# Squared-ReLU attention and adapter mixture on one core: a list scheduler writes the order of every engine, and PSUM is handed out by the bank

## The chip, the core and the metric

The kernel runs on one core of a Trainium2 chip. The metric is the device time in microseconds (us) of one execution. TensorE (PE) multiplies and transposes into PSUM, ScalarE (ACT) and VectorE (DVE) read PSUM and write SBUF, GpSimd (POOL) issues the input transfers and SyncE (SP) the output transfers. PSUM has 8 banks of 512 fp32 values per partition.

## The reference, cut to what matters

```python
# q, k, v: (8, 12, 448, 64); w_gate: (768, 8); A: (8, 768, 16); B: (8, 16, 768)
scores = (1 / sqrt(64)) * q @ k.T            # per batch and head, 448 x 448
attn = maximum(scores, 0) ** 2 / 448
x = (attn @ v), heads side by side           # (3584, 768)
logits = x @ w_gate                          # 8 experts, the best 2 count
w = softmax over the best 2
out = x + sum over the 2 experts of w_e * (x @ A[e]) @ B[e]
```

## The kernel before

Work comes in 8 batches of 3 "quads"; a quad is four heads of one batch, two of them (`g`) on each half of the 128 partitions and two (`sl`) side by side. Sequence positions are split as (p j), so that a step `j` of 7 takes 64 of the 448 keys for all four heads. There are 24 x 7 = 168 steps. A step is:

- `emit_qk(n)` (L228): four 64x64 matmuls of 448 columns into a score tile `s` of two PSUM banks. `ps_s` holds two such tiles.
- `emit_relu(n)` (L238): one ACT instruction over both banks, 128x896, writes `a1`; L240: one DVE product squares it into `a2`.
- `emit_pv(n)` (L252): four matmuls that add `a2` times `v` to `oT`, two banks that are held for the whole quad.

Before a quad, `job_transpose` turns its q and its k (14 PE transposes, L112, and a DVE copy, L119, each). After a quad, `emit_xt` copies `oT` into `xt` (L262 on ACT, L263 on DVE). When the columns of 128 rows are complete, `job_moe` runs for two or three of the 28 row tiles at once: gate logits and the 128 adapter columns `z` (L133), eight short DVE and ACT instructions that make the weights (L145 to L161), `zp` (L166), its transpose `zt` (L175) and copy `zT` (L180), and then for each tile two pieces of output, `o`: identity matmuls that bring `x` itself into the bank (L189), an fp32 matmul with B (L197), a copy to SBUF (512 columns on ACT, L208; 256 on DVE, L210) and two stores by SP (L212).

The order of every engine is the order in which Python emits the instructions. The loop over n at the end fixes it: in step n PE gets QK(n), then a transpose job or one piece of `job_moe`, and then PV(n-2) (`LAG` is 2). In PSUM `misc` has two banks for the transposes and all of `job_moe`, `s` four and `oT` two. What the loop emits, each engine runs strictly in that order, and an instruction waits for the semaphores of what it reads and overwrites.

Loads are issued by POOL, batch 0 by pairs of heads, each later batch as a whole when its buffer comes free. A is loaded by six transfers in runs of 16 floats.

Of the kernel before, what the change touches and what calls it, by code (L numbers as in the profile page):

```python
# [15 lines left out]
PH = 64  # L16


@with_exitstack
def kernel(  # L20
# [21 lines left out]
    NC_ = HH // 2  # L42
    scale = 1.0 / math.sqrt(Dh)
# [3 lines left out]
    loads = ctx.enter_context(tc.tile_pool(name="loads", bufs=3))  # L47
    tpool = ctx.enter_context(tc.tile_pool(name="tpool", bufs=2))
    apool = ctx.enter_context(tc.tile_pool(name="apool", bufs=4))
    mpool = ctx.enter_context(tc.tile_pool(name="mpool", bufs=2))  # L50
    opool = ctx.enter_context(tc.tile_pool(name="opool", bufs=4))
# [8 lines left out]
    identb = const.tile([128, 128], BF16)  # L60

# [5 lines left out]
    )  # L67

    batches = {}

    def load_batch(b, per_quad=False):
        tiles = [
            loads.tile([128, HH, J * Dh], BF16, name=f"{nm}n{b}", tag=f"{nm}n") for nm in "qkv"
        ]
        batches[b] = tiles
        parts = [(2 * c, 2 * c + 2) for c in range(NC_)] if per_quad else [(0, HH)]
        for s0, s1 in parts:
            for t, src in zip(tiles, (qv, kv, vv)):
                for g in range(2):
                    nc.gpsimd.dma_start(  # L80
                        out=t[g * PH : g * PH + PH, s0:s1, :], in_=src[b, g, :, s0:s1, :]
                    )
# [3 lines left out]
    load_batch(0, per_quad=True)  # L86
    nc.sync.dma_start(out=B_sb, in_=moe_B.rearrange("e r d -> (e r) d"))
    load_batch(1)
    nc.gpsimd.dma_start(
        out=awg[:, :, RE:ZW], in_=moe_w_gate.rearrange("(do di) e -> di do e", di=128)  # L90
    )
    for do in range(DO):
        nc.gpsimd.dma_start(
            out=awg[:, do, 0:RE].rearrange("p (e r) -> p e r", e=E),
            in_=moe_A[:, do * 128 : do * 128 + 128, :].transpose([1, 0, 2]),
        )

    quads = [(b, c) for b in range(B) for c in range(NC_)]
    NQ = len(quads)
    qkT = {}  # L100

    def misc(name):
        return ps_m.tile([128, 512], F32, name=name, tag="misc")


    def job_transpose(qi, which):
        b, c = quads[qi]
        src = batches[b][which]
        ps = ps_m.tile([128, J * 128], BF16, name=f"tp{which}_{qi}", tag="misc")
        for j in range(J):  # L110
            for sl in range(2):
                nc.tensor.transpose(  # L112
                    ps[sl * PH : sl * PH + PH, j * 128 : j * 128 + 128],
                    src[:, 2 * c + sl, j * Dh : j * Dh + Dh],
                    identb,
                )
        yield
        sb = tpool.tile([128, J, 2, PH], BF16, name=f"{'qk'[which]}T{qi}", tag=f"{'qk'[which]}T")
        nc.vector.tensor_copy(sb.rearrange("p j a s -> p (j a s)"), ps)  # L119
        qkT[qi, which] = sb  # L120

    def out_rows(m, bp):

        b = 2 * bp + m // J
        return out[b * S : b * S + S, :].rearrange("(p j) f -> j p f", j=J)[m % J]

    def job_moe(bp, tiles_):
        T = len(tiles_)
        c0 = [bp * 2 * S + 128 * i for i in tiles_]
        z = misc(f"z{bp}_{tiles_[0]}")  # L130
        for t in range(T):
            for do in range(DO):
                nc.tensor.matmul(  # L133
                    out=z[:, t * ZW : t * ZW + ZW],
                    lhsT=xt[:, do, c0[t] : c0[t] + 128],
                    rhs=awg[:, do, :],
                    start=(do == 0),
                    stop=(do == DO - 1),
                )
        yield  # L140
        z3 = z[:, : T * ZW].rearrange("p (t w) -> p t w", t=T)
        lg = z3[:, :, RE:ZW]
        mx = mpool.tile([128, 3, 8], F32, name=f"mx{bp}_{tiles_[0]}", tag="mx")
        for t in range(T):
            nc.vector.max(mx[:, t, :], z[:, t * ZW + RE : t * ZW + ZW])  # L145
        sub = mpool.tile([128, 3, E], F32, name=f"sub{bp}_{tiles_[0]}", tag="sub")
        nc.vector.tensor_tensor(
            sub[:, :T], lg, mx[:, :T, 0:1].to_broadcast([128, T, E]), op=ALU.subtract
        )
        w = mpool.tile([128, 3, E], F32, name=f"w{bp}_{tiles_[0]}", tag="w")  # L150
        nc.scalar.activation(w[:, :T], sub[:, :T], ACTF.Exp)
        mask = mpool.tile([128, 3, E], F32, name=f"mask{bp}_{tiles_[0]}", tag="mask")
        nc.vector.tensor_tensor(
            mask[:, :T], lg, mx[:, :T, 1:2].to_broadcast([128, T, E]), op=ALU.is_ge
        )
        yield
        nc.vector.tensor_mul(w[:, :T], w[:, :T], mask[:, :T])
        ws = mpool.tile([128, 3], F32, name=f"ws{bp}_{tiles_[0]}", tag="ws")
        nc.vector.reduce_sum(ws[:, :T], w[:, :T], axis=mybir.AxisListType.X)
        nc.vector.reciprocal(ws[:, :T], ws[:, :T])  # L160
        nc.vector.tensor_tensor(  # L161
            w[:, :T], w[:, :T], ws[:, :T, None].to_broadcast([128, T, E]), op=ALU.mult
        )
        zp = mpool.tile([128, 3, E, R], F32, name=f"zp{bp}_{tiles_[0]}", tag="zp")
        for t in range(T):
            nc.vector.tensor_tensor(  # L166
                zp[:, t],
                z[:, t * ZW : t * ZW + RE].rearrange("p (e r) -> p e r", e=E),
                w[:, t, :, None].to_broadcast([128, E, R]),
                op=ALU.mult,  # L170
            )
        yield
        zt = misc(f"zt{bp}_{tiles_[0]}")
        for t in range(T):
            nc.tensor.transpose(  # L175
                zt[:, t * 128 : t * 128 + 128], zp[:, t].rearrange("p e r -> p (e r)"), identf
            )
        yield
        zT = mpool.tile([128, 3 * 128], F32, name=f"zT{bp}_{tiles_[0]}", tag="zT")
        nc.scalar.copy(zT[:, : T * 128], zt[:, : T * 128])  # L180
        yield
        pend = None
        for t in range(T):
            osb = opool.tile([128, D], F32, name=f"o{bp}_{tiles_[t]}", tag="o")
            for part in range(2):
# [23 lines left out]
                else:  # L209
                    nc.vector.tensor_copy(dst, o[:, : nd * 128])  # L210
                    for hh in range(2):
                        nc.sync.dma_start(  # L212
                            out=out_rows(2 * tiles_[t] + hh, bp),
                            in_=osb[hh * PH : hh * PH + PH, :],
                        )


    sc, at2, oT = {}, {}, {}

    def emit_qk(n):  # L220
# [126 lines left out]
```

## Time and profile before

| | us |
|---|---|
| median of 3 runs (277.43 to 278.75) | 277.51 |
| the profiled execution's own time | 275.26 |
| its span, first to last instruction | 273.5 |
| PE busy | 205.1 |
| ACT busy | 177.7 |
| DVE busy | 169.2 |

The time of an execution holds some work outside the span (275.26 against 273.5). No engine is busy for more than three quarters of the span. A busy figure counts an engine as busy from the start to the end of an instruction, and the start of the next one can lie ahead of that end; where it matters, the distance from start to start is read.

### The profile page before, as it was taken

The page shows a single profiled execution, that of the slowest core. Times are in us where ns is not written, and L with a number is a line of the kernel's source. Part 1 is how long each engine was busy: PE and PEld are TensorE (multiplying, and loading weights), DVE is VectorE, ACT ScalarE, POOL GpSimd, SP SyncE. Part 2 cuts the span into 40 slices and gives each one's busy share as a digit, 9 for nine tenths or more (in the row PEclk, how much of TensorE's full clock was granted, in tenths as well). Part 3 has the DMA queues.
Part 4 walks back from the last instruction along what each step waited for, and adds up shares of the span by engine and source line. Part 5 has one row for each costly group of instructions (what it writes and reads, how often), then busy time and mean ns, then how long its engine had stood idle before and what let it go on. Part 6 is the DMA issues. An engine that isn't in the chain of part 4 may idle for free.

```text
span 273.5 us, 6096 instructions
## 1 busy us (share of the span) xinstructions
PE 205.1 (75%) x2492; PEld 100.3 (37%) x2492; DVE 169.2 (62%) x397; ACT 177.7 (65%) x245; POOL 45.2 (17%) x73
## 2 busy tenths in 40 slices
PE   0877759976795997898697687788686866789762
PEld 0433424433343344434344334334233433334331
DVE  0588866586867657756877767755746666463230
ACT  1488957786786576767777787676736776664120
POOL 8975732101110103001110100000000000000000
PEclk9999997999999599599999999799959979979799
DMA  7999999998193188716692642022200400403244
GB/s 130 186 181 182 112 203 205 220 228 139 21 211 89 9 149 145 119 37 123 128 188 72 112 97 60 2 59 60 59 2 6 111 0 2 115 2 84 89 116 115
DMA packets 31067, 28.51 MB, mean 104 GB/s; under 512 B 8896, under 2 KB 27328, under 8 KB 31040
## 3 DMA queue, kind: packets, MB, share of 16 engines
q0 software_dynamic: 26416, 16.73, 49.3%
q1 hardware_dynamic: 4624, 11.41, 15.4%
q8 instruction: 19, 0.31, 0.5%
q14 instruction: 8, 0.07, 0.1%
HBM read 33.84 MB, written 11.01 MB: 164 GB/s over the span
## 4 chain that ended last, share of the span: by engine, by line
PE 44%; DVE 21%; ACT 19%; issue 8%; POOL 4%; DMA 2%; ACTq 0%; POOLq 0%
ACT a L238 15%; PE o L197 15%; PE oT L252 10%; DVE a L240 9%; PE s L228 7%; PE o L189 6%; ACT o L208 3%; DVE kT L119 3%; DMA qn<-in_q_dram 2%; DVE xt L263 2%; PE tp L112 2%; PE zt L175 2%; DVE zp L166 2%; POOL qn L80 2%; PE z L133 2%
## 5 line engine op out<-in xcount | busy, mean ns | idle before, releaser
L238 ACT ACTIVATE a<-s 128x896 bf16<-128x896 f32 x168 | 148.6, 921 | 43.9 <-PE s L228 42.9
L240 DVE TENSOR_TENSOR a<-a 128x896 bf16<-128x896 bf16 x168 | 103.5, 623 | 76.0 <-ACT a L238 74.7
L252 PE MATMUL oT<-a,vn 64*64 64x448 bf16 x672 | 71.6, 390 | 13.5 <-DVE a L240 4.8
L228 PE MATMUL s<-qT,kT 64*64 64x448 bf16 x672 | 68.0, 381 | 10.9 <-ACT a L238 10.2
L197 PE MATMUL o<-B_sb,zT 128*128 128x512 f32 (+1 forms) x112 | 53.0, 559 | 0.5 <-ACT zT L180 0.5
L252 PEld LDWEIGHTS <-vn 64*64 64x64 bf16 x672 | 23.5, 108 | 61.2 <-issue 49.8
L228 PEld LDWEIGHTS <-kT 64*64 64x64 bf16 x672 | 24.3, 112 | 18.9 <-issue 14.9
L189 PE MATMUL o<-identb,xt 128*128 128x128 bf16 x168 | 20.5, 236 | 12.0 <-ACT o L208 8.3
L208 ACT COPY o<-o 128x512 f32<-128x512 f32 x28 | 16.5, 589 | 16.6 <-PE o L197 16.6
L189 PEld LDWEIGHTS <-xt 128*128 128x128 bf16 x168 | 12.3, 104 | 34.3 <-issue 29.5
L80 POOL DMA_DIRECT2D vn<-in_v_dram x20 | 13.0, 666 | 64.7 <-PE s L228 46.0
L112 PE MATMUL tp<-identb,qn 128*64 128x128 bf16 x336 | 15.8, 241 | 6.6 <-DMA qn<-in_q_dram 6.6
L197 PEld LDWEIGHTS o<-B_sb,zT 128*128 128x128 f32 x112 | 18.8, 210 | 0.8 <-ACT zT L180 0.8
L175 PE MATMUL zt<-identf,zp 128*128 128x128 f32 x28 | 7.2, 354 | 15.2 <-DVE zp L166 15.2
L119 DVE COPY qT<-tp 128x896 bf16<-128x896 bf16 x24 | 14.8, 615 | 5.8 <-PE tp L112 5.8
L210 DVE COPY o<-o 128x256 f32<-128x256 f32 x28 | 11.7, 418 | 10.6 <-PE o L197 10.6
L80 POOL DMA_DIRECT2D qn<-in_q_dram x20 | 13.2, 671 | 30.4 <-PE tp L112 28.6
L112 PEld LDWEIGHTS <-qn 128*64 128x64 bf16 x336 | 11.6, 121 | 15.7 <-issue 8.4
L133 PE MATMUL z<-awg,xt 128*128 128x136 bf16 x168 | 12.7, 223 | 4.3 <-DVE kT L119 2.4
L263 DVE CAST xt<-oT 128x448 bf16<-128x448 f32 x24 | 14.8, 618 | 1.7 <-PE oT L252 1.7
L112 PE MATMUL tp<-identb,kn 128*64 128x128 bf16 x336 | 15.1, 233 | 0.3 <-DMA kn<-in_k_dram 0.3
L119 DVE COPY kT<-tp 128x896 bf16<-128x896 bf16 x24 | 14.8, 618 | 0.6 <-PE tp L112 0.6
(25 smaller groups left out, 89.6 us busy)
## 6 DMA issues: line engine op xcount, KB each, us to landing
out_dram<-o SPq DMA_DIRECT2D x56, 192.0 KB, 2.7
qn<-in_q_dram POOLq DMA_DIRECT2D x14, 336.0 KB, 6.5
kn<-in_k_dram POOLq DMA_DIRECT2D x14, 336.0 KB, 7.5
vn<-in_v_dram POOLq DMA_DIRECT2D x14, 336.0 KB, 6.0
qn<-in_q_dram POOLq DMA_DIRECT2D x6, 112.0 KB, 4.5
kn<-in_k_dram POOLq DMA_DIRECT2D x6, 112.0 KB, 4.5
vn<-in_v_dram POOLq DMA_DIRECT2D x6, 112.0 KB, 4.7
B_sb<-in_moe_B_dram SPq DMA_DIRECT2D x1, 384.0 KB, 3.3
```

The costliest lines, as they stand in the source:

```text
L80: nc.gpsimd.dma_start(out=t[g * PH : g * PH + PH, s0:s1, :], in_=src[b, g, :, s0:s1, :])
L112: nc.tensor.transpose(ps[sl * PH : sl * PH + PH, j * 128 : j * 128 + 128], src[:, 2 * c + sl, j * Dh : j * Dh + Dh], identb,)
L119: nc.vector.tensor_copy(sb.rearrange("p j a s -> p (j a s)"), ps)
L133: nc.tensor.matmul(out=z[:, t * ZW : t * ZW + ZW], lhsT=xt[:, do, c0[t] : c0[t] + 128], rhs=awg[:, do, :], start=(do == 0), stop=(do == DO ...
L189: nc.tensor.matmul(out=o[:, i * 128 : i * 128 + 128], lhsT=xt[:, d0 + i, c0[t] : c0[t] + 128], rhs=identb, start=(i == 0), stop=False, ski ...
L197: nc.tensor.matmul(out=o[:, : nd * 128], lhsT=zT[:, t * 128 : t * 128 + 128], rhs=B_sb[:, d0 * 128 : (d0 + nd) * 128], start=False, stop=True,
L208: nc.scalar.copy(dst, o[:, : nd * 128])
L228: nc.tensor.matmul(out=s[a * PH : a * PH + PH, sl, 0:S].rearrange("p (j s) -> p j s", j=J), lhsT=kT[r0 : r0 + PH, j, a, :], rhs=qT[r0 : r0 ...
L238: nc.scalar.activation(a1, sc[n][:, :, 0:S], ACTF.Relu, scale=relu_scale)
L240: nc.vector.tensor_mul(a2, a1, a1)
L252: nc.tensor.matmul(out=oT[qi][g][sl * PH : sl * PH + PH, 0:S], lhsT=vn[r0 : r0 + PH, 2 * c + sl, j * Dh : j * Dh + Dh], rhs=at2[n][r0 : r0 ...
L263: nc.vector.tensor_copy(xt[:, NC_ + c, b * S : b * S + S], oT[qi][1][:, 0:S])
```

## The change

The loop is gone. Each piece of work becomes an `Op` with an engine (or a choice of ACT and DVE), a duration in a table, its inputs, the buffers it takes and gives back, and the PSUM banks that it wants. `schedule` runs a clock over them and writes down the order in which they would start; the instructions are then emitted in that order, so that it is fixed when the program is built. What moves:

- All of PSUM is one tile of 8 banks. Scores use banks 0 to 3, and each bank is given back by itself: the ReLU becomes two ACT instructions of 448 columns, one for each bank. Banks 4 to 7 serve everything else.
- `DEFER = 6`: the first PV of a quad waits until the square of its last step is there, so that the 7 PVs of a quad come late and close together, and hold their two banks for that long only.
- Buffers: q and k transposes 4 instead of 2, `a2` 8 instead of 4.
- The fp32 matmul with B comes in pieces of 256 columns, which other PE work may stand between. The output copies are all 512 wide, and they, the `xt` and the `zT` copies go to ACT or DVE, whichever the clock finds free.
- The order in which PE changes between attention and other work is weighed with a cost for each change.
- Batch 7 runs as two halves (`UB`) of 224 query columns, so that 42 steps of half the width replace 21, and the first half's rows can be finished ahead of the second's.
- A arrives in one transfer in runs of 96 floats, in another row order; 72 PE matmuls with a selection matrix `sel`, which POOL writes, put it in its place.
- Stores: 63 instead of 56; the last two row tiles are stored in eight pieces of 32 rows.

The core of the diff:

```diff
+SLACK = 0.0
+BANKS = {"s": [0, 1, 2, 3], "m": [4, 5, 6, 7]}
+HOLD = 1
+DEFER = 6
+POOLS = dict(qT=4, kT=4, a1=4, a2=8, zp=2, zT=3, osb=3, w=3)
...
+    def pick(e):
+        c = [o for o in avail[e] if can(o)]
+        if not c:
+            return None
+        if e != "PE":
+            return min(c, key=lambda o: (o.ready + o.rank, seq[id(o)]))
+        att = sorted((o for o in c if o.mode == "64"), key=lambda o: (o.kind != "qk", seq[id(o)]))
+        fill = [o for o in c if o.mode != "64"]
...
+        if mode == "64" and att:
+            return att[0]
+        if fill:
+            f = fill[0]
+            if not att or att[0].kind != "qk" or t + f.dur[e] + switch + 0.55 <= cover + SLACK:
+                return f
+        return att[0] if att else fill[0]
...
+def act(n):
+    return n / 1400.0 + 0.075
...
-    ps_s = ctx.enter_context(tc.tile_pool(name="ps_s", bufs=2, space=bass.MemoryType.PSUM))
-    ps_o = ctx.enter_context(tc.tile_pool(name="ps_o", bufs=1, space=bass.MemoryType.PSUM))
-    ps_m = ctx.enter_context(tc.tile_pool(name="ps_m", bufs=2, space=bass.MemoryType.PSUM))
...
+    ps = psum.tile([128, 8, 512], F32)
...
+    UB = [1] * (B - 1) + [2]
...
+        r0 = op(ACT, act(W), AL, lambda: fn(0), deps=[qk_ops[n]], after=prev, kind="relu",
+                take=("a1",), free=[(qk_ops[n], 0)])
+        r1 = op(ACT, act(W), AL, lambda: fn(1), deps=[qk_ops[n]], after=r0, kind="relu", free=[(qk_ops[n], 1)])
+        return [r0, r1]
...
+        wait = [sq_ops[n], loaded[b, 2, c]]
+        if j == 0:
+            wait += [sq_ops[n + DEFER]]
+        o = op(PE, 0.194 / UB[b], PL, fn, mode="64", kind="pv", deps=wait, after=pv_ops.get(n - 1),
+               banks=("m", 2) if j == 0 else None, give=("a2",))
...
-        nc.scalar.activation(a1, sc[n][:, :, 0:S], ACTF.Relu, scale=relu_scale)
...
+        o = op(PE, 0.194 / UB[b], PL, fn, mode="64", kind="qk", deps=[tp_ops[b, c, 0], tp_ops[b, c, 1]],
+               after=qk_ops.get(n - 1), banks=("s", 2, "adjacent")[: 2 + (UB[b] > 1)], give=("qT", "kT") if n == last_use[b, c] else ())
...
+        def mm():
+            for x in range(3):
+                for i in range(DO):
+                    y0 = 128 * (d0 + x) - i + DO - 1
+                    for rhs, lo, hi in ((a_raw[:, :, i, :], 0, RE), (g_raw[:, i, :], RE, ZW)):
+                        nc.tensor.matmul(
+                            out=bank(m)[:, x * ZW + lo : x * ZW + hi],
+                            lhsT=sel[:, y0 : y0 + 128],
+                            rhs=rhs,
...
+                        nc.tensor.matmul(
+                            out=o[:, off + h0 * 128 : off + (h0 + 2) * 128],
+                            lhsT=T["zT", g0][:, zi * 128 : zi * 128 + 128],
+                            rhs=B_sb[:, (d0 + h0) * 128 : (d0 + h0 + 2) * 128],
...
+                while r < 128:
+                    b, x = divmod(pair[t] * 128 + r, S)
+                    pu = PH // UB[b]
+                    u, y = divmod(x, J * pu)
+                    j, p = divmod(y, pu)
+                    m = min(pu - p, 128 - r)
+                    nc.sync.dma_start(
+                        out=outv[b, j, u * pu + p : u * pu + p + m], in_=osb[r : r + m, t, :]
...
+    for c in range(NC_):
+        for w in range(3):
+            loaded[0, w, c] = load(0, w, 2 * c, 2 * c + 2, [])
+    sel_op = op(("POOL",), 1.5, 0.1, sel_fn)
+    a_load = op(("POOL",), 2.0, 3.0, aw_fn, kind="load")
+    aw_ops = [aw_place(x, [a_load, sel_op]) for x in range(2)]
...
-    LAG = 2
...
+    for o in schedule(ops):
+        o.fn()
```

The rows below are the program's order on three engines, of before and of the change, at the same place of the work. In the names the batch and tile numbers are those that the build gave.

ACT of before, from the third step of quad 7 on (`a_51` is step 51 of 168):

```order
L238 ACTIVATE a_51_1267<-s_1253 128x896
L238 ACTIVATE a_52_1297<-s_1277 128x896
L208 COPY o_3_1260<-o_0_3_1261 128x512
L238 ACTIVATE a_53_1317<-s_1305 128x896
L238 ACTIVATE a_54_1340<-s_1325 128x896
L208 COPY o_4_1333<-o_0_4_1334 128x512
```

ACT of the change, at the same steps:

```order
L406 ACTIVATE a_51_1290<-ps 128x448 x2
L406 ACTIVATE a_52_1314<-ps 128x448 x2
L406 ACTIVATE a_53_1333<-ps 128x448 x2
L456 CAST xt<-ps 128x448
L618 COPY osb_1353<-ps 128x512
L406 ACTIVATE a_54_1355<-ps 128x448 x2
```

Each ReLU is now two instructions, and copies stand where the scheduler's clock found room.

PE of before around one piece of output in quad 7 (`s_1253` are the scores of step 51, `a_49` the squares of step 49; weight loads and repeats left out):

```order
L228 MATMUL s_1253<-qT_1094,kT_1152 64x448
...
L189 MATMUL o_0_3_1261<-identb,xt 128x128
...
L197 MATMUL o_0_3_1261<-B_sb,zT_3_1213 128x512
...
L252 MATMUL oT_7_1271<-a_49_1217,vn_168 64x448
...
L228 MATMUL s_1277<-qT_1094,kT_1152 64x448
```

PE of the change at the same place (the scores are again those of step 51, `a_42` the squares of step 42):

```order
L585 MATMUL ps<-identb,xt 128x128
...
L593 MATMUL ps<-B_sb,zT_1031 128x256
L379 LDWEIGHTS kT_1_971
L379 MATMUL ps<-qT_1_899,kT_1_971 64x448
...
L434 MATMUL ps<-a_42_1131,vn_833 64x448
```

The matmul with B that stands between two score steps has 256 columns instead of 512, and the PV that follows QK(51) is that of step 42 instead of 49.

SP of before, the last stores (a row is one tile of 128 rows):

```order
L212 DMA out_dram<-o_2_4013 64x768 x2
L212 DMA out_dram<-o_3_4063 64x768 x2
L212 DMA out_dram<-o_4_4078 64x768 x2
L212 DMA out_dram<-o_5_4128 64x768 x2
L212 DMA out_dram<-o_6_4143 64x768 x2
```

SP of the change, the last stores (a tile `osb` is a pair of row tiles):

```order
L636 DMA out_dram<-osb_3920 64x768 x4
L636 DMA out_dram<-osb_4069 64x768 x4
L636 DMA out_dram<-osb_4190 64x768 x4
L636 DMA out_dram<-osb_4228 64x768
L636 DMA out_dram<-osb_4228 32x768 x6
L636 DMA out_dram<-osb_4257 32x768 x8
```

Eight stores instead of two now stand behind the last output copy.

## Rows read from the trace of the kernel before

**Rows 1.** The page, busy time by engine, with its share of the span.

```profile
PE 205.1 (75%) x2492; PEld 100.3 (37%) x2492; DVE 169.2 (62%) x397; ACT 177.7 (65%) x245; POOL 45.2 (17%) x73
```

**Rows 2.** Windows: busy us by engine; the last columns PEclk, DMA share, GB/s.

```profile
9.94:247.40 237.46, 186.30 (x2366) 89.90 (x2363) 160.42 (x366) 171.20 (x233) 36.03 (x53) 0.93 0.67 102
247.40:273.50 26.10, 16.22 (x96) 8.75 (x95) 7.34 (x29) 5.22 (x11) 0.00 (x0) 0.93 0.40 106
...
14.20:23.00 8.80, 6.32 (x104) 2.94 (x97) 7.12 (x13) 8.06 (x11) 5.64 (x9) 1.00 1.22 188
...
143.60:164.00 20.40, 15.60 (x225) 7.94 (x220) 14.81 (x35) 16.19 (x24) 1.31 (x2) 1.00 0.46 94
```

**Rows 3.** Waits of ACT and PE: total us, times, the longest.

```profile
ACT a L238 <- PE s L228: 42.9, 53, 7.9
ACT w L151 <- DVE sub L147: 17.5, 12, 1.7
ACT o L208 <- PE o L197: 16.6, 15, 2.3
...
PE zt L175 <- DVE zp L166: 15.2, 12, 2.0
```

**Rows 4.** Timeline from 141.8 us: start, duration, idle before it.

```profile
141.80 1.08 PE L197 MATMUL o<-B_sb,zT 128*128 128x512 f32 x2
...
143.02 0.36 PE L228 MATMUL s<-qT,kT 64*64 64x448 bf16 x4
...
143.43 0.92 ACT L238 ACTIVATE a<-s 128x896 bf16<-128x896 f32 x1 [0.83 <-PE s L228]
```

**Rows 5.** Timeline, ACT back to back; last, the group of casts.

```profile
14.23 4.16 ACT L238 ACTIVATE a<-s 128x896 bf16<-128x896 f32 x5 [0.50 <-PE s L228]
...
144.24 0.53 ACT L262 CAST xt<-oT 128x448 bf16<-128x448 f32 x1
...
144.66 0.59 ACT L208 COPY o<-o 128x512 f32<-128x512 f32 x1
...
145.14 0.94 ACT L238 ACTIVATE a<-s 128x896 bf16<-128x896 f32 x1
...
L262 ACT CAST xt<-oT 128x448 bf16<-128x448 f32 x24 | 12.9, 538 | 1.8 <-PE oT L252 1.8
```

**Rows 6.** Timeline of PE, pieces of work back to back at the higher clock.

```profile
140.35 0.29 PE L189 MATMUL o<-identb,xt 128*128 128x128 bf16 x2
...
141.06 0.38 PE L252 MATMUL oT<-a,vn 64*64 64x448 bf16 x4
...
146.21 0.36 PE L228 MATMUL s<-qT,kT 64*64 64x448 bf16 x4
...
146.50 0.58 PE L112 MATMUL tp<-identb,kn 128*64 128x128 bf16 x14
...
147.01 0.38 PE L252 MATMUL oT<-a,vn 64*64 64x448 bf16 x4
...
148.78 0.87 PE L133 MATMUL z<-awg,xt 128*128 128x136 bf16 x12 [0.81 <-DVE kT L119]
...
149.80 0.36 PE L228 MATMUL s<-qT,kT 64*64 64x448 bf16 x4
...
149.99 0.36 PE L252 MATMUL oT<-a,vn 64*64 64x448 bf16 x4
```

**Rows 7.** The end: the last copy, and the stores' issue and landing.

```profile
268.46 0.42 DVE L210 COPY o<-o 128x256 f32<-128x256 f32 x1 [1.55 <-PE o L197]
...
L212 SPq DMA_DIRECT2D out_dram<-o x56: 466/562/1311, 49.8 to 269.5; - x56
...
DMA to landing us min/median/max: 2.6/2.7/5.9
```

**Rows 8.** Timeline of PE: attention matmuls back to back at the lower clock.

```profile
200.34 0.58 PE L228 MATMUL s<-qT,kT 64*64 64x448 bf16 x4
200.72 0.58 PE L252 MATMUL oT<-a,vn 64*64 64x448 bf16 x4
```

More of the change, by code (lines that the diff above doesn't have):

```diff
@@ L67 @@
     )
[L69 to L82, printed above, removed]
+    UB = [1] * (B - 1) + [2]
@@ L84, with new @@
+    GATE, EVAC, XT, LEAD = -0.4, -0.3, 0.0, 5
+    outv = out.rearrange("(b p j) f -> b j p f", b=B, j=J)
     make_identity(nc, identf)
     nc.vector.tensor_copy(identb, identf)
[L86 to L92, printed above, removed]
+    ops = []
+    T = {}
+    def new(pool, key, shape, dt):
+        T[key] = sb_pools[pool].tile(shape, dt, name="_".join(str(x) for x in key), tag=pool)
+        return T[key]
@@ new lines, in op, with bank, evac, load @@
+    def op(*a, **kw):
+        o = Op(*a, **kw)
+        ops.append(o)
+        return o
+    def bank(o, i=0):
+        return ps[:, o.banks[i], :]
+    PE, DVE, ACT, ANY = ("PE",), ("DVE",), ("ACT",), ("ACT", "DVE")
+    DL, AL, PL = 0.084, 0.135, 0.165
+    def evac(n, fn, **kw):
+        o = op(ANY, {"ACT": act(n), "DVE": dve(n)}, {"ACT": AL, "DVE": DL}, None, **kw)
+        o.fn = lambda: fn(nc.scalar.copy if o.eng == "ACT" else nc.vector.tensor_copy)
+        return o
+    def load(b, w, s0, s1, deps):
+        def fn():
+            if (b, w) not in T:
+                nm = f"{'qkv'[w]}n"
+                T[b, w] = loads.tile([128, HH, J * Dh], BF16, name=f"{nm}{b}", tag=nm)
+            for g in range(2):
+                nc.gpsimd.dma_start(
+                    out=T[b, w][g * PH : g * PH + PH, s0:s1, :],
+                    in_=(qv, kv, vv)[w][b, g, :, s0:s1, :],
+                )
+        return op(("POOL",), max(1.2, (s1 - s0) * 0.64), 2.0, fn, deps=deps, kind="load")
@@ new lines, in sq, with fn, pv @@
+    def sq(n):
+        W = width(order[n][0])
+        def fn():
+            a2 = new("a2", ("a2", n), [128, 2, W], BF16)
+            nc.vector.tensor_mul(a2, T["a1", n], T["a1", n])
+        return op(DVE, dve(2 * W, 1.92), DL, fn, deps=relu_ops[n], take=("a2",), give=("a1",))
+    def pv(n):
+        b, u, c, j = order[n]
+        W = width(b)
+        def fn():
+            vn = T[b, 2]
+            for g in range(2):
+                r0 = g * PH
+                for sl in range(2):
+                    nc.tensor.matmul(
+                        out=bank(head, g)[sl * PH : sl * PH + PH, :W],
+                        lhsT=vn[r0 : r0 + PH, 2 * c + sl, j * Dh : j * Dh + Dh],
+                        rhs=T["a2", n][r0 : r0 + PH, sl, :],
+                        start=(j == 0),
+                        stop=(j == J - 1),
+                    )
+        wait = [sq_ops[n], loaded[b, 2, c]]
[3 more added lines that the diff above has]
+               banks=("m", 2) if j == 0 else None, give=("a2",))
+        head = o if j == 0 else pv_ops[n - j]
+        return o
```

633 lines of the change are left out of this document (430 added, 203 removed).

## Prediction

> **What bounds the kernel now.** I read the busy times first [rows 1]. PE has 205.1 of 273.5 us, ACT 177.7, DVE 169.2: no engine fills the span, so it is made of waits between engines. Next come the windows [rows 2]. The kernel has three stretches: a head of 9.94 us to the first ReLU, in which the first q and k arrive; a middle of 237.46 us, from the first ReLU to the end of the last one; and 26.1 us behind it. In the middle ACT, which has the 168 ReLUs, is busy for 171.20 us, that is 72%, and idle for 66.
>
> The waits say for what [rows 3]. ACT waits 42.9 us for QK, and further for pieces of the adapter work that stand ahead of the next ReLU in its fixed order: 17.5 us for `sub`, 16.6 us for `o`. PE stands still 15.2 us, in 12 pieces, at `zt`, which the loop emits one step behind `zp`; while it stands, the next QK stands behind it.
>
> One step shows how a QK comes late [rows 4]. A fp32 matmul with B starts on PE at 141.80, PV follows it, QK starts only at 143.02, and the ReLU starts 0.41 us later, at 143.43, after 0.83 us of idle ACT. How much delay the two score tiles forgive can be worked out. Two ReLUs start 0.81 us apart when nothing holds them ((4.16 - 0.92) / 4, [rows 5]), and one lasts 0.92. Let one start at 0: its tile is free at 0.92, a QK issued then is ready at 1.33 (0.41 later), and ACT would take it at 1.62. So QK may come 0.29 us late, and each piece of other work in front of it takes more.
>
> **The change, part by part.**
>
> *The ring of scores.* With banks given back one by one, the first bank is free when the first half of a ReLU ends. A 448-column instruction lasts 0.538 [rows 5], so its QK pair is ready at 0.95, while ACT, after the other three halves, comes back to the bank at 4 x 0.43 = 1.72. The slack is 0.77 us instead of 0.29. The pieces that stand in front of a QK shrink: four identity matmuls and half a B matmul take about 0.24 + 0.49 plus two changes of work at 0.1, 0.93 us, instead of 1.4. What is left over the slack is about 0.15 us, where it was over 1 us. The waits for `sub`, `zt` and `o` go too, as far as the order puts the waiting instruction late enough; the order leaves several ReLUs between them.
>
> *The price of the split.* The trace has no 448-column ReLU. From below: a 448-column cast is followed 0.42 us later by the next instruction, a 512-column copy 0.48 later [rows 5]. From above: nothing overlaps, 0.538 each. A line through 0.48 at 512 columns and 0.81 at 896 gives 0.43 at 448, and I take it, since those starts are back to back on the same engine. Two halves then cost 0.86 instead of 0.81. ACT's own work is 336 x 0.43 = 144.5, 29 `xt` casts (a fifth of them half as wide) 11, 22 output copies 10.6, six `zT` and ten exponentials 4.4: 170.5 us, against 167 before by the same prices. Some 3 us of it fall behind the last ReLU.
>
> The Trainium skill has a rule that speaks against the split ("ScalarE: Activation LUTs", section "What ACT_TABLE_LOAD costs"): an ACTIVATE with immediate scale and bias takes 186 ns and 0.833 ns for each column, and neighbours overlap by about 93 ns. By it a half costs 0.466 and a whole 0.839, so ACT's total would be about 12 us more than mine; the trace has 0.81 for the whole, below the rule.
>
> *PE.* By starts [rows 6] a QK or PV is 0.19 (149.80 to 149.99), a change between attention and other work 0.10 (146.21 to 146.50, less 0.19), a set of 14 transposes 0.41 (to 147.01, less one change), a 128-column matmul 0.06 (12 in 0.87 with the last one's length), a 256-column B 0.49 (140.35 to 141.06, less two identities and a change). `zt`, fp32 with 128 columns, I put at half of B, 0.25. The changed program has 147 full and 42 half QKs and as many PVs (64.3), 48 transposes (19.7), 408 narrow matmuls, 72 of them the new placement of A (24.5), 84 B pieces (41.2), 28 `zt` (7) and 240 changes of work (24): 180.7 us, 6 more than before. About 163 of it lie in the middle, under ACT's 167. DVE's work stays as it was; its count of busy time is 169.2 with overlaps [rows 1].
>
> *The middle.* ACT's work of 167 us sets its length, if ACT is fed. How well can it be fed? In the stretch from 14.2 to 23.0 us no adapter work stands in front of QKs, only transposes of 0.51, and ACT is busy 8.06 of 8.80 us, 92% [rows 2]. With pieces of at most 0.9 and a slack of 0.77 I expect about that: 167 / 0.92 = 181.5. Two places belong to PE: the third quad, which gets the placement of A and the first transposes of batch 1 (8.6 us of PE by the prices above, 6.3 of ACT), and the last five half quads (26.4 of PE in all, 21 of ACT). They add 2 + 5. Middle: 188.5 us, against 237.46.
>
> *The head* keeps its 9.94: the order of the first loads is unchanged. POOL's work for `sel` and the single load of A lie behind batch 0's loads, where six loads of A lay before; batch 1 is first needed in the third quad, some 15 us later. If that cover is gone, the first transposes of batch 1 wait as long as the load is late, a few us.
>
> *The end.* After the last ReLU: square 0.6, PV 0.2; then PE has 7 `zt`, 24 `z`, 42 identities and 21 B pieces, 1.7 + 1.4 + 2.5 + 10.3 = 15.9; 1.0 for waits at `z` and `zT`; a 512-column copy 0.7. Then the stores. One issue on SP takes 0.56, and landing 2.7; before, the last issue came at 269.5, landed at 272.2, and the span ended 1.3 later [rows 7]. Now eight issues stand behind the last copy, and the seven of the tile pair before are just through (0.3): 0.3 + 7 x 0.56 + 2.7 + 1.3 = 8.2, where the row of 268.46 has 4.6 behind its copy. Sum 26.6, against 26.1: finishing the first half of batch 7 early buys about what the small stores cost.
>
> *Sum:* 9.94 + 188.5 + 26.6 = 225 us of span, 48.5 less. With the 1.76 us outside the span the profiled execution would take 226.8; the median before stands at 277.51 / 275.26 = 1.008 of its profiled time, so 228.5.
>
> **Rivals.**
>
> *ACT pays in full for the second instruction.* Against it speak the starts in [rows 5]. If half of the gap to 0.538 were paid, a half would cost 0.47 to 0.48, the middle (3 + 336 x 0.475 + 20) / 0.92 + 7, some 205, and the time 245. If all: 267. The Trainium skill's rule of above, 0.466, would give 242.
>
> *ACT stays hungry.* The order is fixed by a table in which a half ReLU takes 0.395, less than my 0.43, so that engines run late against each other in a way that the order does not know. In the best 20 us that hold adapter work now, ACT is busy 16.19 of 20.40, 79% [rows 2]. At that share the middle is 167 / 0.79 + 7 = 218, and the time 258.
>
> *Slower: the PV burst stops the ring.* The first PV of a quad waits for the square of its seventh step. On PE a QK stands behind it, and on DVE the square stands behind copies that wait for PE. `a2` has 8 buffers, so a PV that is late stops DVE one quad later, then ACT. A stop like that at `zt`, 15.2 / 12 = 1.3 us [rows 3], once in each of 24 quads' worth of work costs 31 us and leaves 259. It decides from 2.0 us a quad, 49 in all. For it speaks that one wait of ACT for QK lasted 7.9 us [rows 3]; against it that in the order the burst is broken by QKs after at most seven PVs, and that the square which opens it stands behind one or two copies only.
>
> *The change doesn't do what it says.* If waits on the one PSUM tile were kept for the tile and not for the bank, every engine would stand in line, and the time would not fall. The order gives each half ReLU a wait of its own on PE, which speaks against it.
>
> A lower clock is in the upper bound: at the lower level a QK takes 0.38 instead of 0.19 [rows 8], and the middle has a mean of 0.93 now [rows 2]. I expect no less, with fewer stops of PE.
>
> **How the numbers follow.** The forecast has 0.64, the dearer split 0.13, the hungry ACT 0.14, the burst 0.06, the change without effect 0.03. Below: with 0.42 a half and both ACT and PE above 95% the middle cannot be much under 172, which gives 212. Above: the range takes in the dearer split (245) and most of the way to the hungry ACT, 253. A measurement tells 0.5% from no change; all cases but the last two are far on the fast side, and the burst ends there too in part: faster 0.93, same 0.02, slower 0.05.
>
> **What would show it.** ACT ReLUs that start 0.42 to 0.44 apart when back to back; ACT busy over 90% between first and last ReLU; its wait for QK under 15 us instead of 42.9; the PE wait at `zt` gone outside the end; the end near 26 us. I am wrong if halves start 0.48 or more apart, if ACT's share stays near 79%, or if PE waits for squares by more than 1 us a quad.

## The result and the profile after

The changed kernel takes 216.19 us (median of 4 runs, 215.29 to 216.73), the kernel before 277.73 beside it on the same chip: a ratio of 0.778, 95% interval 0.774 to 0.781. The time lies in the predicted range, near its low end: 12 us below the 228.5 forecast. In the sessions of the runs below the kernel before took 270.94 to 281.10 us, the longer ones at a lower granted clock (0.955 at 270.94, 0.908 at 281.10), so that a ratio to it can be off by some 2%, and the changed kernels are compared by their times. The profiled execution took 216.73 us, with a span of 215.0.

The busy times of the changed kernel (us, share of the span, instructions), from its page, to be held against [rows 1]:

```profile
span 215.0 us, 6965 instructions
PE 196.5 (91%) x2788; PEld 121.4 (56%) x2788; DVE 166.5 (77%) x387; ACT 177.6 (83%) x404; POOL 49.2 (23%) x82
```

The busy time of each engine is nearly that of before (PE has 8.6 us less, ACT 0.1, DVE 2.7); the span shrank around it. Where it shrank is seen in the windows: head, middle from the first ReLU to the end of the last, and end, as in [rows 2]; then the ten microseconds in which A is put in place, and the long stretch after it.

```profile
0.00:10.38 10.38, 2.55 (x36) 1.68 (x36) 1.48 (x3) 1.29 (x2) 9.25 (x21) 1.00 0.87 143
10.38:190.65 180.27, 177.07 (x2609) 106.53 (x2606) 152.52 (x347) 173.87 (x397) 39.99 (x62) 0.99 0.72 129
190.65:215.00 24.35, 16.84 (x149) 13.19 (x147) 12.50 (x38) 2.43 (x8) 0.00 (x0) 0.94 0.58 155
23.00:33.00 10.00, 10.00 (x200) 7.04 (x198) 7.41 (x15) 7.64 (x18) 9.20 (x15) 0.83 1.22 185
33.00:157.00 124.00, 122.26 (x1761) 71.91 (x1755) 112.68 (x255) 123.46 (x287) 18.43 (x28) 1.00 0.75 136
```

The middle fell from 237.46 to 180.27 us, 57.2 of the 58.5 us that the span lost: the head is 0.44 us longer, the end 1.75 shorter. From 33 to 157 us ACT (the fourth of the five busy times) is busy for 123.46 of 124.00 us. The waits say the same; these rows answer to [rows 3]:

```profile
ACT a L406 <- PE ps L379: 10.7, 4, 8.3
ACT a L404 <- PE ps L379: 2.1, 8, 0.4
ACT osb L618 <- PE ps L593: 3.8, 6, 1.6
ACT wt L503 <- DVE sub L497: 2.1, 2, 1.8
PE ps L551 <- DVE zp L530: 0.4, 2, 0.2
```

L406 is the split ReLU, L404 the ReLU of the half steps of batch 7. Together ACT waits 12.8 us for QK, 12 times, where it waited 42.9 us, 53 times; 8.3 of the 12.8 us are the start, before the first scores. ACT's 17.5 us at `sub` are down to 2.1, both pieces behind the last ReLU, and PE's 15.2 us at `zt` to 0.4.

The timeline of ACT from 113 us, start and length, shows the price of the split ReLU and answers to [rows 5]:

```profile
113.03 2.25 ACT L406 ACTIVATE a<-ps 128x448 bf16<-128x448 f32 x4
114.74 1.02 ACT L618 COPY osb<-ps 128x512 f32<-128x512 f32 x1
115.20 2.31 ACT L406 ACTIVATE a<-ps 128x448 bf16<-128x448 f32 x4
116.91 0.97 ACT L563 COPY zT<-ps 128x384 f32<-128x384 f32 x1
```

Four halves take 1.71 us from the first one's start to that of the copy behind them, both times: 0.43 us each. A copy of 512 columns takes 0.46.

The end answers to [rows 7]. The groups of PE in 190.65 to 215.0 us (count, then busy us and mean ns), and from the timeline of DVE the last copy:

```profile
L593 PE MATMUL ps<-B_sb,zT 128*128 128x256 f32 x46 | 13.0, 398 | 0.0
L585 PE MATMUL ps<-identb,xt 128*128 128x128 bf16 x44 | 4.9, 219 | 0.0
L473 PE MATMUL ps<-awg,xt 128*128 128x136 bf16 x24 | 1.7, 223 | 0.0
L551 PE MATMUL ps<-identf,zp 128*128 128x128 f32 x7 | 1.1, 281 | 0.2 <-DVE zp L530 0.2
```

```profile
207.92 0.69 DVE L618 COPY osb<-ps 128x512 f32<-128x512 f32 x1 [0.51 <-PE ps L593]
```

The trace has two records for each fp32 piece of B, so 23 pieces stand behind the last ReLU. PE does them without a stop. From the end of the last copy, 208.61, to the end of the span are 6.4 us of stores.

### The profile page after: what moved, and what is told of

Same layout as the page of the kernel before. It is cut to its first block, busy times and chain, and to the rows that moved or that the text cites. A ratio compares the mean times of both kernels' runs of the same rounds, so it can differ in the third digit from the quotient of the medians.

```text
span 215.0 us, 6965 instructions
## 1 busy us (share of the span) xinstructions
PE 196.5 (91%) x2788; PEld 121.4 (56%) x2788; DVE 166.5 (77%) x387; ACT 177.6 (83%) x404; POOL 49.2 (23%) x82
## 4 chain that ended last, share of the span: by engine, by line
PE 58%; ACT 20%; DVE 9%; issue 5%; DMA 3%; POOL 1%; DVEq 0%; POOLq 0%; ACTq 0%
ACT a L406 18%; PE ps L379 16%; PE ps L593 16%; PE ps L434 9%; PE ps L351 6%; PE ps L585 5%; DVE a L421 4%; PE ps L473 4%; DMA kn<-in_k_dram 2%; PE ps L311 2%; PE ps L551 1%; DVE zp L530 1%; ACT xt L456 1%; DMA out_dram<-osb 1%; DVE xt L456 1%
## 5 line engine op out<-in xcount | busy, mean ns | idle before, releaser
L406 ACT ACTIVATE a<-ps 128x448 bf16<-128x448 f32 x294 | 138.8, 682 | 11.4 <-PE ps L379 10.7
L421 DVE TENSOR_TENSOR a<-a 128x896 bf16<-128x896 bf16 (+1 forms) x189 | 103.6, 569 | 24.8 <-ACT a L406 13.0
L379 PE MATMUL ps<-qT,kT 64*64 64x448 bf16 (+1 forms) x756 | 77.3, 351 | 2.7 <-DVE kT L359 0.7
L593 PE MATMUL ps<-B_sb,zT 128*128 128x256 f32 x168 | 52.8, 409 | 0.0
L434 PE MATMUL ps<-a,vn 64*64 64x448 bf16 (+1 forms) x756 | 47.2, 336 | 0.1
L593 PEld LDWEIGHTS ps<-B_sb,zT 128*128 128x128 f32 x168 | 26.1, 190 | 4.2 <-issue 3.3
L404 ACT ACTIVATE a<-ps 128x448 bf16<-128x448 f32 x42 | 21.0, 551 | 2.3 <-PE ps L379 2.1
L585 PE MATMUL ps<-identb,xt 128*128 128x128 bf16 x168 | 18.8, 221 | 0.3 <-DVE xt L456 0.2
L456 ACT CAST xt<-ps 128x448 bf16<-128x448 f32 (+1 forms) x29 | 17.0, 604 | 2.0 <-PE ps L434 2.0
L618 ACT COPY osb<-ps 128x512 f32<-128x512 f32 x22 | 15.0, 682 | 3.9 <-PE ps L593 3.8
L351 PEld LDWEIGHTS <-qn 128*64 128x64 bf16 x336 | 10.8, 114 | 11.8 <-DMA qn<-in_q_dram 7.3
L271 POOL DMA_DIRECT2D kn<-in_k_dram x24 | 15.4, 657 | 7.7 <-DMA qn<-in_q_dram 3.7
```

What stands on the lines that cost most here:

```text
L271: nc.gpsimd.dma_start(out=T[b, w][g * PH : g * PH + PH, s0:s1, :], in_=(qv, kv, vv)[w][b, g, :, s0:s1, :],)
L351: nc.tensor.transpose(o[sl * PH : sl * PH + PH, j * 128 : j * 128 + 128], T[b, w][:, 2 * c + sl, j * Dh : j * Dh + Dh], identb,)
L379: nc.tensor.matmul(out=bank(o, sl)[a * PH : a * PH + PH, : width(b)].rearrange("p (j s) -> p j s", j=J), lhsT=kT[r0 : r0 + PH, j, a, :], r ...
L404: nc.scalar.activation(a1, two(qk_ops[n], W), ACTF.Relu, scale=relu_scale)
L406: nc.scalar.activation(a1[:, sl], bank(qk_ops[n], sl)[:, :W], ACTF.Relu, scale=relu_scale)
L421: nc.vector.tensor_mul(a2, T["a1", n], T["a1", n])
```

## The experiments

Three theories were set against one another. The prediction's own: ACT is fed because a score bank comes back with half a ReLU, so that a QK may come later. Second: the order itself feeds ACT, by where it puts waits and pieces. Third: what was added around it (late burst of PVs, buffers, smaller pieces) lets the engines run ahead of one another.

**One whole ReLU again.** Only the split is undone: QK takes two adjacent banks, one instruction frees both.

```diff
-               ... banks=("s", 2, "adjacent")[: 2 + (UB[b] > 1)], ...
+               ... banks=("s", 2, "adjacent"), ...
...
-        if UB[b] > 1:
+        if True:
             return [op(ACT, act(2 * W), AL, lambda: fn(None), ...
```

> The change with its ReLU whole again: one ACT instruction of 128x896 that gives both score banks back at its end; the scheduler, its other rules and the half steps of the last batch stay. Theory 1 (the ring's slack of 0.77 us is what feeds ACT): the slack falls back to 0.29 us, and ACT's idle time between first and last ReLU grows from 6 to over 20 us, though ACT has 7 us less work: 224 to 235 us. Theory 2 (the written-out order alone feeds ACT, the split does nothing or costs): 208 to 217 us, ACT idle still under 8.

Measured: 214.62 us (213.83 to 214.67). Its middle and end, and its wait for QK:

```profile
10.12:185.80 175.68, 167.38 (x2578) 100.75 (x2574) 150.99 (x340) 165.04 (x249) 39.72 (x62) 1.00 0.74 132
185.80:212.90 27.10, 19.75 (x182) 15.89 (x179) 14.11 (x44) 2.54 (x8) 0.00 (x0) 0.95 0.56 147
```

```profile
ACT a L404 <- PE ps L379: 15.1, 16, 8.1
```

Without the split ACT waits for QK a little more (15.1 us, 16 times, against 12.8), and is idle in the middle for 10.6 us instead of 6.4, between what the two theories expected. But it has 8.8 us less to do there, and the middle is 4.6 shorter. The ring by the bank is not what feeds ACT; the prediction's chief step falls.

**The split ring alone, in the kernel before.**

```diff
-ps_s = ... bufs=2       # two tiles of two banks
+ps_s = ... bufs=4       # four tiles of one bank
...
-nc.scalar.activation(a1, sc[n][:, :, 0:S], ACTF.Relu, scale=relu_scale)
+for sl in range(2):
+    nc.scalar.activation(a1[:, sl], sc[n][sl][:, 0:S], ACTF.Relu, scale=relu_scale)
```

> The kernel before with one part of the change alone: four one-bank score tiles and the ReLU in two instructions of 448 columns, each bank free by itself; order, PV lag, pieces and buffers as before. Theory 1 (ring slack): a good part of ACT's 42.9 us of waiting for QK goes, some 20 us, and the time falls to 250 to 262 us. Theory 2 (the order): the waits stay where the fixed order puts them, and ACT has 7 us more work: 275 to 284 us.

Measured: 279.76 us (277.63 to 281.69), where the kernel before had a median of 278.18 beside it: no gain. That it is slower is not shown, since the ratio of 1.027 (1.020 to 1.034) sets a clock of 0.921 to 0.932 against one of 0.943 to 0.955. Waits of this kernel:

```profile
ACT a L239 <- PE s L228: 38.5, 54, 7.9
ACT w L151 <- DVE sub L147: 17.3, 12, 1.7
ACT o L208 <- PE o L197: 17.3, 17, 2.2
```

They stand where [rows 3] has them. In the fixed order the finer ring buys 4 us of waiting for QK, and ACT is busy for 188.2 us instead of 177.7. With the run before, the first theory is out from both sides.

**The PV burst.** `DEFER = 6` becomes 2, so that the first PV of a quad waits for the third square and not the seventh.

> The change with DEFER 2 instead of 6: the first PV of a quad waits for the square of its third step only, and its two banks are held for most of the quad. Theory 1 (ring slack): PV's place matters little, 216 to 222 us. Theory 3 (the late burst frees two of the four other banks for transposes and adapter work, and that is what lets the order flow): ACT idles at banks that are not free, 228 to 245 us.

Measured: 218.15 us (217.47 to 218.72). The late burst is worth some 2 us by the medians, and it is no danger either.

**B in one piece.** The matmuls with B become 512 columns wide where four column blocks are due, as before the change.

```diff
-for h0 in range(0, nd, 2):
+for h0 in (0,):
 (and the matmul and its price in the table over nd column blocks)
```

> The change with the fp32 matmul of B in one piece of up to 512 columns with its identities, 1.2 us long instead of 0.73. Theory 1 (slack 0.77 against the length of the piece in front of a QK): 56 - 28 = 28 pieces overrun the slack by up to 0.5 us more each, 219 to 228 us. Theory 2 (the order alone): within 1 us of 216.

Measured: 218.14 us (216.34 to 220.43). Its runs overlap those of the changed kernel; whether the smaller pieces are worth 2 us or nothing stays open.

**About the buffers of before.** The transposes of q and k have 3 buffers each, where the kernel before had 2; the others are as there.

```diff
-DEFER = 6
-POOLS = dict(qT=4, kT=4, a1=4, a2=8, zp=2, zT=3, osb=3, w=3)
+DEFER = 2
+POOLS = dict(qT=3, kT=3, a1=4, a2=4, zp=2, zT=2, osb=2, w=2)
...
-    sbx = ... bufs=3
+    sbx = ... bufs=2
```

> The changed kernel with about the buffers of before: q and k transposes 3 each instead of 4, a2 4 instead of 8, zT 2, output rows 2, gate weights 2, small tiles 2, and DEFER 2, which a2 needs. The order is written anew for them. If the order itself is the gain (each engine finds its input there because the waiting instruction is placed late), 214 to 222 us. If the extra buffers are the gain, because they let engines run ahead of one another, 230 us and more, with ACT's wait for QK back above 20 us.

Measured: 217.44 us (217.05 to 217.93). But for the third buffer of the transposes, the buffers in SBUF are not the gain. The third theory is left with PSUM alone, whose four banks for everything but scores were not tried smaller in the new order.

**The kernel before without its gate waits.** The exponential reads a constant instead of `sub`, `zt` transposes a constant instead of `zp`. The gate's weights are thereby left out of the output; each engine's instructions stay.

```diff
-nc.scalar.activation(w[:, :T], sub[:, :T], ACTF.Exp)
+nc.scalar.activation(w[:, :T], cst[:, :T], ACTF.Exp)
...
-    zt[:, t * 128 : ...], zp[:, t].rearrange("p e r -> p (e r)"), identf
+    zt[:, t * 128 : ...], czp, identf
```

> The kernel before, in which the exponential reads a constant tile instead of sub, and zt transposes a constant instead of zp; so the gate's weights are left out of the output, and the work on each engine stays. ACT no longer waits 17.5 us at sub, nor PE 15.2 at zt. If such waits in a fixed order are what the middle of before is made of, the time falls by some 20 to 30 us, to 248 to 258. If they only hide another bound (the fixed order of pieces in front of QK), 270 or more.

Measured: 252.61 us (251.83 to 254.46). That is 25.6 us less than the median of before beside it (278.24), and 18.6 less than its shortest run (271.25), whose clock, 0.955, comes nearest to the 0.962 to 0.969 here. The middle, and behind it the waits that are left:

```profile
10.19:230.43 220.24, 179.13 (x2365) 87.09 (x2362) 159.23 (x365) 171.03 (x233) 36.05 (x53) 0.97 0.74 110
```

```profile
ACT a L242 <- PE s L232: 46.1, 57, 8.2
ACT o L212 <- PE o L201: 13.7, 15, 1.6
```

Two kinds of wait, 12 of each [rows 3], stand for 18.6 to 25.6 of the 61.5 us that the change gains. Not all of the 25.6 is the wait itself: the granted clock in the middle is 0.97, where [rows 2] has 0.93. As an estimate, if PE's speed set all of the middle, the missing clock is 0.07 x 237.46 = 16.6 us before and 0.03 x 220.24 = 6.6 here, so up to 10 of the 25.6 us may be PE's speed.

**The same waits moved by hand.** The loop of before puts the exponential, `zT` and the wide output copies behind the ReLU of their step (`late`), `zt` one step later, and starts the next group in the step in which one ends. Nothing is left out.

```diff
-nc.scalar.copy(dst, o[:, : nd * 128])
+late.append(lambda dst=dst, o=o: nc.scalar.copy(dst, o[:, :512]))
...
         yield
+        yield
         zt = misc(...)
...
             emit_relu(n)
+        flush()          # what stands in late
```

> The kernel before, with its loop and all its pieces, in which five kinds of waiting instructions stand later by hand: the exponential, the copy zT and the 512-column output copies come behind the ReLU of their step instead of ahead of it, zt comes one step later, and to pay for that step the next group of row tiles starts in the step in which the last one ends. Nothing is left out. If the waits at sub, o, zt and zT (17.5, 16.6, 15.2 and 10.3 us) are what the fixed order cost, most of them go and the time is 232 to 252 us. If the wait only moves to the next ReLU, which then stands without its QK, 265 us or more.

Measured: 280.15 us (278.67 to 282.94), ratio 1.014 (1.004 to 1.025). The moved waits shrank and the time did not:

```profile
ACT a L240 <- PE s L230: 68.6, 61, 8.4
ACT o L210 <- PE o L199: 9.7, 6, 2.8
PE o L191 <- DVE kT L120: 8.4, 7, 1.2
PE o L191 <- DVE qT L120: 7.3, 5, 1.5
ACT w L152 <- DVE sub L148: 7.1, 8, 1.4
PE zt L177 <- DVE zp L167: 7.0, 8, 2.0
```

ACT's wait at `sub` went from 17.5 to 7.1 and at `o` from 16.6 to 9.7, PE's at `zt` from 15.2 to 7.0. In exchange ACT waits 68.6 us for QK instead of 42.9, and PE 15.7 us, at the output pieces, for the copies of transposes out of the two `misc` banks. So the expectation held for the rival. The steps show more. From the starts of the 168 ReLUs in the traces the mean distance to the next ReLU, by what PE has in that step between QK and PV:

```
PE's piece in the step       before   no gate waits   moved by hand
none (58, 58, 59 steps)       0.86        0.98            1.10
transposes (46)               1.49        1.30            1.25
z (10)                        1.83        1.63            1.97
zt (10)                       2.62        1.56            1.62
o, 4 blocks (22, 22, 21)      2.06        1.93            2.18
o, 2 blocks (21)              1.35        1.35            1.67
```

Moving the waits by hand made the steps with `zt` and with transposes shorter and all others longer. Without the gate waits a step with no piece takes 0.98 (half of them 0.81, ACT's own), a step with one 1.3 to 1.9. There PE's work from one QK to the next is uneven: it is busy for 0.55 of 0.85 us in steps with no piece, 1.15 of 1.15 with transposes, 1.86 of 2.03 with four blocks. As an estimate, the larger of the two engines' busy times in each kind of step adds up to some 198 us, where PE's alone adds up to 178 and the middle is 220. So the unevenness, which nothing in the loop balances, explains about half of what stays when the waits go; the rest is not traced.

**Pieces without regard to ACT.** In the changed kernel a piece goes ahead of a waiting QK only if ACT's queue covers it. Here the test always passes.

```diff
-SLACK = 0.0
+SLACK = 10.0
```

> The changed kernel with SLACK at 10 instead of 0: the test that a piece of other work goes ahead of a waiting QK only when ACT has work enough to cover it is always passed, so that all pieces that are ready go in a row. If that test is what keeps ACT fed, ACT's wait for QK rises from 11 us to 30 and more and the time to 230 to 250 us. If four score banks and the late pieces keep it fed without the test, 214 to 222.

Measured: 242.6 us (241.82 to 244.33), 26.4 above the changed kernel. First the middle, then ACT's waits for QK, then PE and ACT from 63 us by the timeline:

```profile
10.15:222.73 212.58, 195.65 (x2710) 121.83 (x2707) 176.59 (x392) 165.34 (x378) 39.80 (x62) 0.98 0.66 122
```

```profile
ACT a L406 <- PE ps L379: 41.9, 15, 8.3
ACT a L404 <- PE ps L379: 8.2, 7, 3.1
```

```profile
63.63 0.58 PE L351 MATMUL ps<-identb,qn 128*64 128x128 bf16 x14
64.14 1.59 PE L473 MATMUL ps<-awg,xt 128*128 128x136 bf16 x24
65.67 0.58 PE L351 MATMUL ps<-identb,kn 128*64 128x128 bf16 x14
66.18 0.57 PE L379 MATMUL ps<-qT,kT 64*64 64x448 bf16 x8
66.59 0.22 ACT L503 ACTIVATE wt<-sub 128x24 f32<-128x24 f32 x1 [1.14 <-DVE sub L497]
66.72 5.32 ACT L406 ACTIVATE a<-ps 128x448 bf16<-128x448 f32 x12
```

Three pieces in a row keep PE from QK for 2.6 us; ACT runs dry and starts its next ReLU at 66.72. (The row puts its idle time down to `sub`, which comes from the second of the three pieces; the QK starts at 66.18.) Banks and buffers are as in the changed kernel: the test is what keeps ACT's wait for QK at 12.8 us and not 50.1. Without it the kernel is still 34 us faster than the one before (276.98 beside it).

**A table that knows no chain.** The nine steps from `z` to `zp` take no time in the table, so that `exp` and `zt` are ordered close behind their inputs.

```diff
-o_max = op(DVE, 0.075 * n, DL, f_max, ...
+o_max = op(DVE, 0.0, 0.0, f_max, ...
 (and so on to o_zp)
```

> The changed kernel, in whose table the nine steps from z to zp (max, sub, exp, mask, products, sum, reciprocal, zp) take no time; so the order puts the exponential right behind sub and zt right behind z's weights. Nothing else differs: same instructions, buffers, banks and pieces. If the gain comes from waiting instructions that stand late enough, the waits of ACT at sub and of PE at zt come back, ten groups at 1 to 2 us on each of the two engines: 224 to 240 us. If the even pieces, banks and buffers are the gain, 213 to 219.

Measured: 218.55 us (217.62 to 220.88). ACT waits 11.4 us at `sub` instead of 2.1, 7.1 of them in one piece, PE 3.6 at `zt`; the time rises by 2 us, not by 8 to 24.

```profile
198.80 0.21 ACT L503 ACTIVATE wt<-sub 128x16 f32<-128x16 f32 x1 [7.12 <-DVE sub L497]
```

This piece and one of 2.54 at 202.03 stand behind the last ReLU, which ends at 191.31; in the middle are only 1.8 us. The gate's waits don't come back there with a wrong price for its chain, so foresight of that chain is not what removes them. Which property of the order does is not settled by these runs.

**A loaded the old way,** by six transfers, without the 72 matmuls (`aw_place`) and `sel`.

> The changed kernel with A loaded as before, by six transfers in runs of 16 numbers, and without the 72 matmuls that place it and without sel. Order written anew. If the placement costs what its work on PE is (72 matmuls, 4.3 us, in a stretch where ACT was busy 6.64 of 9.00 us), the time falls by 2 to 3 us. If the short runs cost more (packets under 512 bytes go from 3360 back to some 8900, and POOL issues five transfers more ahead of batch 1), it rises by 2 to 5 us.

Measured: 217.55 us (216.99 to 218.43): no gain, though PE has about 3 us less to do (the placement's two runs of 36 matmuls take 1.7 and 1.5 us in the changed kernel; the 4.3 us expected come from a price of 0.06 each).

```profile
9.78:188.08 178.30, 174.68 (x2521) 101.81 (x2517) 150.91 (x342) 173.83 (x398) 43.05 (x66) 1.00 0.78 130
188.08:216.00 27.92, 20.18 (x166) 16.01 (x163) 13.96 (x39) 2.69 (x7) 0.00 (x0) 0.96 0.53 142
```

The middle is 2.0 us shorter, and the end 3.6 longer: 30 pieces of B stand behind the last ReLU, not 23.

**Batch 7 whole.** `UB = [1] * B`.

> The changed kernel with batch 7 whole: 21 steps of 448 columns instead of 42 of 224, and 56 stores instead of 63. The order is written anew. The prediction has it that finishing the first half early buys about what the small stores cost: then 214 to 219 us. If the halves are worth the whole of the row tiles that they let through early (about half of the 16 us of PE behind the last ReLU), 220 to 226.

Measured: 214.67 us (214.39 to 215.72). Again middle and end trade:

```profile
10.17:179.65 169.48, 166.75 (x2377) 98.00 (x2373) 150.53 (x321) 167.07 (x384) 39.96 (x62) 1.00 0.73 127
179.65:212.60 32.95, 25.15 (x215) 19.86 (x212) 17.33 (x48) 3.03 (x8) 0.00 (x0) 0.96 0.62 168
```

ACT is busy for 98.6% of this middle. Yet what the middle gains, 10.8 us, the end gives back but for 2.2: 34 pieces of B are left for it. The two runs lead to another reading of what limits the new kernels; middle and end of each, from its first to its last ReLU and from there to the end of the span:

```
                      middle    end    sum    pieces of B in the end
changed kernel        180.27   24.35  204.6   23
whole ReLU            175.68   27.10  202.8   27 (53 records)
old load of A         178.30   27.92  206.2   30
batch 7 whole         169.48   32.95  202.4   34
no regard to ACT      212.58   17.27  229.9    6
```

The reading: when ACT is fed, its work sets the middle, and whatever of PE's work found no room under it is left for the end. The sum hardly moves, since it is PE's work. If that is so, only a cheaper PE helps.

**A cheaper PE.** The whole ReLU again, with B and `zT` rounded to bf16, and the last eight stores issued by SP and ACT in turn.

```diff
-    zT = new("zT", ("zT", g0), [128, 3 * 128], F32)
+    zT = new("zT", ("zT", g0), [128, 3 * 128], BF16)
...
-    rhs=B_sb[:, (d0 + h0) * 128 : (d0 + h0 + 2) * 128],
+    rhs=B_bf[:, (d0 + h0) * 128 : (d0 + h0 + 2) * 128],
...
-    prev = op(PE, 0.485 + ...
+    prev = op(PE, 0.115 + ...
...
+    eng = nc.scalar if p0 + 2 == NT and k_ % 2 else nc.sync
```

> The run with whole ReLUs, in which B and zT are rounded to bf16, so that the 84 pieces of B take about 0.12 us of PE each instead of 0.49 (31 us less in all), and in which every second one of the last eight stores is issued by ACT instead of SP. The table has the new price of B, and the order is written anew. If PE is what the written-out order is now limited by (190 of 213 us busy with whole ReLUs), ACT's work of about 165 us in the middle becomes the limit: at 96% a middle of 172, the end shorter by some 8 us of PE and 2 of issues, 198 to 204 us in all. If what is left is waiting, which a cheaper B doesn't touch, 209 to 214, of which the shorter end is 2 to 4 us.

Measured: 201.94 us (201.41 to 202.26), ratio to before 0.726 (0.724 to 0.729): the fastest version here, 7% ahead of the changed kernel. Middle and end, PE's wait for banks that ACT gives back, and the last copy by the timeline of DVE:

```profile
10.14:186.14 176.00, 157.50 (x2634) 96.83 (x2633) 155.72 (x361) 168.67 (x263) 40.02 (x63) 1.00 0.80 144
186.14:199.60 13.46, 4.86 (x48) 3.33 (x40) 4.40 (x15) 1.15 (x4) 0.00 (x0) 0.78 0.46 133
```

```profile
PE ps L380 <- ACT a L405: 13.5, 35, 1.3
193.84 0.69 DVE L619 COPY osb<-ps 128x512 f32<-128x512 f32 x1 [0.91 <-PE ps L594]
```

The middle is that of the whole ReLU (176.00 against 175.68), with ACT busy for 96%. All of the gain is in the end, 13.46 against 27.10 us, where 6 pieces of B are left. Some of it belongs to the stores: from the end of the last copy, 194.53, to the end of the span are 5.1 us, where the whole ReLU and the changed kernel have 6.4. So most of the end was PE's surplus; with it gone ACT is the bound, and PE waits for it 13.5 us, where the whole ReLU has 6.0 such us and the changed kernel 0.7.

## Why the prediction was right in time and wrong in its chief step

**The head, the end, the prices: right.** The head has 10.38 us for 9.94, the end 24.35 for 26.6. Behind the last ReLU PE has 7 `zt`, 24 `z`, 44 identities and 23 pieces of B, forecast as 7, 24, 42 and 21; the stores take 6.4 us instead of 8.2, which is most of the difference. Half a ReLU costs 0.43, as taken from starts, and the rule of the Trainium skill ("ScalarE: Activation LUTs", section "What ACT_TABLE_LOAD costs") was rightly set aside: an estimate by its 0.466 a half would make four of them 1.86 us, and the trace has 1.71. That the halves of batch 7 buy about what they cost held too: without them it is 214.67 us, with them 216.19, and the ratios to before agree (0.780, interval 0.772 to 0.787, and 0.778).

**The middle: mis-sized.** The forecast was 167 us of ACT work at 92%, 181.5, and 7 for two places that PE owns. By the same prices 180.27 - 7 = 173.3 us hold those 167: a share of 96%. The best stretch of before was no ceiling; there too the order was fixed by the loop. The two places cost 2.4 and 3.4 us of idle ACT, where 2 and 5 were forecast: from 23 to 33 us ACT is busy for 7.64 of 10.00, and from 157 us to the last ReLU for 30.28 of 33.65; in between it hardly waits.

**The ring of scores: the step that failed.** The prediction says: "The slack is 0.77 us instead of 0.29", and lets pieces of 0.93 almost fit it. The split without the order gave nothing (279.76 us), the order without the split lost nothing (214.62 us). The runs put two other causes in its place. One is the rule in `pick` that weighs each piece against ACT's queue: without it 26.4 us are lost. In the kernel before, nothing lets PE's short steps pay for its long ones. The other is the waits for the gate inside the fixed order, which cost the kernel before 18.6 to 25.6 us, up to 10 of the 25.6 by the clock; the prediction named them, but gave them no time of their own. The two were measured in different kernels, and their sum, 45 to 52 of 61 us, is no proof that nothing else acts: four shared PSUM banks and the free choice of ACT or DVE for the copies were never taken out by themselves. That a hand-made later place for the same waits gained nothing fits this: in the fixed order the wait came back at the next QK (68.6 us instead of 42.9).

**The rivals.** The dearer split and the waits for one PSUM tile are refuted by the starts of 0.43 us and by ACT's 123.46 of 124.00 us. (With all of the gap paid, the prediction's own sum gives 269 us, not 267.) The hungry ACT at 79% did not come, and is what the kernel without the cover test shows (165.34 of 212.58 us, 78%; 242.6 us). The burst that stops the ring did not come either: with the burst and without it the times are 216.19 and 218.15.

**Not foreseen:** that middle and end trade. The prediction summed ACT's middle and PE's end as two separate terms, with 163 us of PE's work under 167 of ACT's. By busy time PE was the fuller of the two, 177.07 of 180.27 us against 173.87. The terms are joined through PE's work: what the order cannot place under ACT goes to the end, so that savings of ACT, or of PE in one place, come back there in part or whole.

## What to carry to other kernels

Count, for each step of a fixed loop, the work of both engines: where heavy and light steps alternate, the loop pays at least the larger of the two each time; placing each piece by how much the fed engine has in its queue was worth 26.4 us here. When a written-out order fills one engine, look at what is left over behind its last instruction: what was saved in the middle came back there, and only less work on the other engine shortened their sum. And undo a suspected cause in both kernels: the finer ring looked like the reason until it was taken out of one and put into the other.

## What was not expected of the hardware

In the profile of the changed kernel the granted clock is 0.83 from 23 to 33 us. PE goes there from QK without a stop to 36 of the 72 small matmuls that place A; in their midst, from about 24.2 us, the start distance of a pair grows from 0.08 to 0.14 us, and 24 PV matmuls behind them take 2.37 us. That is about the 0.38 for each four of [rows 8], the lower of the clock's two levels (1.2 and 2.4 GHz). From its timeline of PE:

```profile
24.04 0.22 PE L311 MATMUL ps<-a_raw,sel 128*128 128x128 bf16 x1
24.12 0.23 PE L311 MATMUL ps<-a_raw,sel 128*128 128x128 bf16 x1
24.35 0.27 PE L311 MATMUL ps<-a_raw,sel 128*128 128x128 bf16 x1
24.49 0.27 PE L311 MATMUL ps<-a_raw,sel 128*128 128x128 bf16 x1
25.44 2.37 PE L434 MATMUL ps<-a,vn 64*64 64x448 bf16 x24
```

With batch 7 whole PE does the same placement in the same ten microseconds, and the window has the clock at 1.00:

```profile
23.00:33.00 10.00, 9.88 (x211) 7.16 (x209) 8.75 (x17) 9.12 (x22) 9.68 (x16) 1.00 1.11 162
```

ACT gets 9.12 us of work there instead of 7.64. So the lead of 1.5 us that the runs with whole ReLUs and with batch 7 whole have over the changed kernel may be this alone; that these versions are faster in themselves is not shown. Without the cover test this window has 0.83 too, with `DEFER = 2` 0.94, in the other runs of the changed kernel 1.00; what decides it stays open.
